# An attention and gate kernel: the projection's copies issued ahead of the scaling of o, head 0's copies of q and k made by engines instead of DMA, TensorE run on dummy matmuls during the first loads

## The chip, the cores and the metric

The kernel runs on one core of a Trainium2 chip. The metric is the time of one execution on the device, in microseconds (us). The core has five engines that run their own instruction queues in order: TensorE (PE; its weight loads are shown as PEld), VectorE (DVE), ScalarE (ACT), GpSimd (POOL) and SyncE (SP). Queues wait for one another by semaphores.

## The reference

`xn = layernorm(x)` with x of 2048 x 640. Attention over 32 heads of width 192 with cached k and v of 2048 rows, then a product with a gate that comes from a SwiGLU block on the same xn:

```python
def _A_ref(x, k_cache, v_cache, wq, wo):
    q = (x @ wq).reshape(B, Sq, 32, 192).transpose(0, 2, 1, 3)
    scores = einsum("bhqd,bhkd->bhqk", q, k_cache) * 192 ** -0.5
    o = einsum("bhqk,bhkd->bhqd", softmax(scores), v_cache)
    return o.transpose(0, 2, 1, 3).reshape(B, Sq, 32 * 192) @ wo
...
xn = _layernorm(A_x)
s = _A_ref(xn, k_cache, v_cache, wq, wo)
g = silu((silu(xn @ w1) * (xn @ w3)) @ w2)
return A_x + s * g
```

## The kernel before

Instructions stand on each engine in the order in which the program issues them. The work is a stream of (head h, block qb of 512 queries, pair p of key tiles): 32 x 4 x 8 steps. A step issues the scores two steps ahead and the values of its own pair. At the end of a block the kernel projects q of the next head for the same queries. Head 0 has no head in front of it, so its q is normalized and projected inside its own blocks.

```python
def project(h, qb, half):          # half 1 first, then half 0
    ...
    ps = ps_st.tile([P, 1024], F32, tag="st2", name="ps")     # one of TWO slots, shared with the scores
    for c in range(DC):
        nc.tensor.matmul(ps[:, 0:512], lhsT=w, rhs=xnT[:, c, qs], ...)
    if half:
        nc.scalar.copy(out=qAB[:, 1, qs], in_=ps[:, 0:512])
    else:
        nc.vector.tensor_copy(out=qAB[:, 0, qs], in_=ps[:, 0:512])
    nc.gpsimd.dma_start(out=qC[0:64, half, qs], in_=qAB[64:P, half, qs])
    if half == 0:
        nc.gpsimd.dma_start(out=qC[64:P, 0, qs], in_=qAB[0:64, 0, qs])

def values(n):
    ...                            # 16 matmuls into obank; behind the last pair of a block:
    nc.scalar.copy(out=osum[:], in_=ov[:, 0, :, 0:DH + 1])
    nc.vector.tensor_tensor(out=osum[:], in0=ov[:, 1, :, 0:DH + 1], in1=osum[:], op=ALU.add)
    nc.vector.reciprocal(out=rl, in_=osum[:, :, DH])
    nc.vector.tensor_tensor(out=ostage[...], in0=osum[:, :, 0:DH], in1=rl..., op=ALU.mult)

for n, (h, qb, p) in enumerate(stream):
    scores(n + 2)
    values(n)
    if h == 0 and qb + 1 < NQB:
        if p == 0 and qb > 0:
            ln_stats(qb + 1)       # VectorE: mean and variance of four tiles of x
        if p == NPAIR // 2 - 1:
            ln_norm(qb + 1)        # VectorE xn, TensorE transposes into a score slot, ScalarE copies to xnT
        if p == NPAIR - 3:
            project(0, qb + 1, 1)
            project(0, qb + 1, 0)
    if h + 1 < H:
        ...
        if p == NPAIR - 1:
            project(h + 1, qb, 1)
            project(h + 1, qb, 0)
    ...
```

The scores use the 192 rows of q and k as three rounds of 64 rows on both halves of the array. So some halves of q and k are needed on the other 64 partitions as well: these copies are qC and KC, and they are made by DMA. The other names in the views: `xn` is the normalized x and `pst` and `xnT` its transposes, `ps` a projection and `st` the scores (both in PSUM, the memory that TensorE writes to), `obank` the sums of the values, `osum` the addition of their two halves at the end of a block, `ostage` the scaled result.

## Time and profile before

| | before |
|---|---|
| time, median of 3 runs | 2080.41 us |
| span of the profiled run | 2077.2 us |
| TensorE busy | 1980.5 us (95%) |
| step of a steady block (osum addition to osum addition) | 13.38 us |
| first values matmul | 32.76 us |
| head 0's first three blocks | 20.6, 23.7, 23.8 us |

The first is the page of the profile: the line of the span, TensorE's line in the table of busy time (us, share, instructions), and the chain of work that ended last, by engine.

```profile
span 2077.2 us, 56883 instructions
...
PE 1980.5 (95%) x25838; PEld 1350.0 (65%) x25969; DVE 520.1 (25%) x850; ACT 1279.7 (62%) x1401; POOL 336.7 (16%) x575
...
PE 69%; DVE 16%; ACT 7%; issue 6%; DMA 1%; ACTq 0%; DVEq 0%; POOL 0%
```

VectorE is busy for a quarter of the span only, yet a sixth of the chain runs through it. Such a pair of numbers says: look for a short piece of VectorE work that TensorE waits for, over and over. It is found in the timeline at the end of a block (start us, duration us, engine, line, operation, output<-inputs, and in brackets the idle time of that engine just before and what ended it):

```profile
703.02 1.24 PE L293 MATMUL ps<-xnT,wq 128*128 128x512 bf16 x5
703.17 0.96 DVE L373 TENSOR_TENSOR osum<-obank,osum 128x772 f32<-128x772 f32 x1 [9.89 <-ACT osum L372]
...
704.17 0.18 DVE L375 RECIPROCAL rl_all<-osum 128x4 f32<-128x4 f32 x1
...
704.38 0.96 DVE L376 TENSOR_TENSOR ostage<-osum,rl_all 128x768 bf16<-128x768 f32 x1
...
704.85 0.83 PE L361 MATMUL obank<-vt_112,pT_11373 64*128 64x193 bf16 x16
...
705.26 0.68 DVE L297 CAST qAB<-ps 128x512 bf16<-128x512 f32 x1
...
705.99 0.37 PE L332 MATMUL st_11474<-qAB,KA 64*128 64x512 bf16 x1 [0.32 <-DVE qAB L297]
...
706.64 0.85 PE L361 MATMUL obank<-vt_112,pT_11398 64*128 64x193 bf16 x16
```

The projection is done near 704.2, but VectorE takes the reciprocal and scales o first, and casts qAB from 705.26 to 705.94. The next scores need the slot that the cast empties; they start at 705.99. The two lines of values are 1.79 us apart, where pairs in the middle of a block are 1.315 us apart. So 0.47 us are lost, once a block.

Head 0, next. The waits of TensorE from the start to the end of the first block, and in the second and third (who waited for whom, total us, times, longest us):

```profile
PE pst L276 <- DVE xn L273: 10.4, 2, 10.1
PE st_232 L332 <- DMA qC<-qAB: 6.2, 1, 6.2
PE st_232 L332 <- DMA KC<-KB: 4.0, 1, 4.0
PE st_460 L332 <- DMA qC<-qAB: 1.9, 1, 1.9
...
```

```profile
PE pst L276 <- DVE xn L273: 3.1, 4, 1.3
PE st_1062 L332 <- DMA qC<-qAB: 1.8, 1, 1.8
PE st_764 L332 <- DMA qC<-qAB: 1.8, 1, 1.8
PE st_764 L332 <- DVE qAB L297: 0.8, 1, 0.8
PE st_1062 L332 <- DVE qAB L297: 0.8, 1, 0.8
...
```

And head 0's first four blocks by windows of time: window, its length, busy us (and instructions) of PE, PEld, DVE, ACT and POOL, then the clock granted to TensorE as a share of full speed, DMA share, GB/s.

```profile
32.80:53.40 20.60, 17.35 (x206) 11.55 (x205) 1.54 (x4) 11.73 (x12) 2.66 (x5) 0.89 0.42 71
53.40:77.10 23.70, 18.95 (x215) 11.98 (x216) 9.71 (x25) 12.84 (x14) 4.68 (x8) 0.93 0.07 17
77.10:100.90 23.80, 19.02 (x215) 11.93 (x216) 9.73 (x24) 12.84 (x14) 4.68 (x8) 0.93 0.08 18
100.90:114.30 13.40, 13.03 (x187) 8.88 (x186) 3.31 (x6) 10.00 (x11) 4.19 (x6) 1.00 0.49 94
```

The clock is below 1.00 in the first three. After the wait for qC the score matmuls last about 0.6 us each instead of 0.38: TensorE has fallen back to half speed for a while (the granted clock is 0.50 from 47.64 to 51.06 us).

### The profile page before, as it was taken

Reading aid. Unit: us, or ns where it says so; the run is one execution under the profiler, and the core shown is the slowest. Engines: PE = TensorE matmul, PEld = TensorE weight load, DVE = VectorE, ACT = ScalarE, POOL = GpSimd, SP = SyncE. Lnnn points to the kernel's source line nnn. Section 1 sums busy time; section 2 is a strip of 40 time slices with the busy share of each in tenths; the row PEclk is TensorE's granted clock in tenths of the full one; section 3 lists DMA queues with packets and bytes.
Section 4 is the critical chain, followed back from the end, with each engine's and each line's share of the span. In section 5 each row is a group of like instructions: output and inputs, shape, how many; then the busy total and the mean of one; then the engine's idle time right before and its main releaser. Section 6 shows DMA issues by size and latency. Waiting matters only on the chain.

```text
span 2077.2 us, 56883 instructions
## 1 busy us (share of the span) xinstructions
PE 1980.5 (95%) x25838; PEld 1350.0 (65%) x25969; DVE 520.1 (25%) x850; ACT 1279.7 (62%) x1401; POOL 336.7 (16%) x575
## 2 busy tenths in 40 slices
PE   5899999999999999999999999999999999999998
PEld 2466666666666666666666666666666666567776
DVE  2422222222222222222222222222222222521111
ACT  3577777777777777777777777777777777220000
POOL 2111111111111111111111111111111110000000
PEclk8999999999999999999999999999999999999999
DMA  8033333433233323353433233232323230827772
GB/s 155 18 64 96 65 96 66 95 65 93 64 96 65 95 65 95 66 133 88 95 65 95 66 74 84 59 86 62 82 65 88 65 88 6 236 45 143 147 148 56
DMA packets 361848, 178.48 MB, mean 86 GB/s; under 512 B 307584, under 2 KB 348288, under 8 KB 361600
## 3 DMA queue, kind: packets, MB, share of 16 engines
q1 hardware_dynamic: 335984, 114.96, 25.6%
q0 software_dynamic: 23312, 57.18, 11.3%
q8 instruction: 205, 3.36, 0.7%
q10 hardware_dynamic: 2304, 2.62, 0.5%
q14 instruction: 43, 0.35, 0.1%
HBM read 54.66 MB, written 27.79 MB: 40 GB/s over the span
## 4 chain that ended last, share of the span: by engine, by line
PE 69%; DVE 16%; ACT 7%; issue 6%; DMA 1%; ACTq 0%; DVEq 0%; POOL 0%
PE obank L361 25%; PE ps_s L102 10%; DVE osum L373 6%; ACT osum L372 5%; DVE ostage L376 4%; DVE qAB L297 4%; PE ps_f L499 3%; DVE rl_all L375 1%; PE ps_gu L470 1%; PE ps_gu L473 1%; PE ps L293 1%; DVE stats L258 0%; DMA KC<-KB 0%; DMA qC<-qAB 0%; ACT xnT L278 0%
## 5 line engine op out<-in xcount | busy, mean ns | idle before, releaser
L373 DVE TENSOR_TENSOR osum<-obank,osum 128x772 f32<-128x772 f32 x128 | 123.1, 962 | 1264.4 <-ACT osum L372 1264.4
L298 POOL DMA_DIRECT2D qC<-qAB x256 | 136.4, 533 | 1372.9 <-ACT qAB L295 1170.5
L102 PE MATMUL ps_s<-wo_sb,oT 128*128 128x256 bf16 (+1 forms) x1536 | 210.5, 301 | 2.2 <-issue 2.2
L102 PEld LDWEIGHTS <-oT 128*128 128x128 bf16 x1536 | 150.7, 98 | 61.7 <-issue 3.9
L332 PEld LDWEIGHTS <-KC 64*128 64x128 bf16 x1024 | 96.3, 94 | 111.4 <-DMA KC<-KB 4.5
L293 PE MATMUL ps<-xnT,wqB 128*128 128x512 bf16 x513 | 154.8, 384 | 8.0 <-ACT xnT L278 1.3
L293 PE MATMUL ps<-xnT,wq 128*128 128x512 bf16 x640 | 159.4, 380 | 0.0
L333 PEld LDWEIGHTS <-KA 64*128 64x128 bf16 x1024 | 96.1, 94 | 59.7 <-issue 59.7
L332 PEld LDWEIGHTS <-KA 64*128 64x128 bf16 x1024 | 96.3, 94 | 58.3 <-issue 54.2
L376 DVE TENSOR_TENSOR ostage<-osum,rl_all 128x768 bf16<-128x768 f32 x128 | 122.6, 958 | 4.4
L293 PEld LDWEIGHTS <-wq 128*128 128x128 bf16 x640 | 62.8, 98 | 76.1 <-issue 1.1
L333 PEld LDWEIGHTS <-KB 64*128 64x128 bf16 x1024 | 96.9, 95 | 12.7 <-issue 12.7
L372 ACT COPY osum<-obank 128x772 f32<-128x772 f32 x128 | 101.9, 796 | 0.9 <-PE obank L361 0.9
L332 PEld LDWEIGHTS <-KB 64*128 64x128 bf16 x1024 | 96.5, 94 | 0.3 <-issue 0.3
L333 PEld LDWEIGHTS <-KC 64*128 64x128 bf16 x1024 | 96.6, 94 | 0.0
L293 PEld LDWEIGHTS <-wqB 128*128 128x128 bf16 x640 | 52.4, 98 | 67.6 <-issue 22.0
L297 DVE CAST qAB<-ps 128x512 bf16<-128x512 f32 x128 | 87.5, 683 | 23.5 <-PE ps L293 23.5
L295 ACT CAST qAB<-ps 128x512 bf16<-128x512 f32 x128 | 75.1, 586 | 13.8 <-PE ps L293 4.7
L300 POOL DMA_DIRECT2D qC<-qAB x128 | 67.1, 524 | 0.2 <-issue 0.2
L107 DVE SCALAR_TENSOR_TENSOR tmp<-ps_s,hT 128x384 f32<-128x384 f32 (+1 forms) x32 | 15.6, 487 | 181.3 <-PE ps_s L102 181.3
L499 PE MATMUL ps_f<-w_all,hT 128*128 128x384 bf16 (+1 forms) x384 | 52.3, 299 | 0.0
L98 POOL DMA_DIRECT2D xt<-in_A_x_dram x16 | 8.6, 540 | 257.6 <-DVE res L110 257.6
(9264 smaller groups left out, 5479.7 us busy)
## 6 DMA issues: line engine op xcount, KB each, us to landing
qC<-qAB POOLq DMA_DIRECT2D x384, 64.0 KB, 1.9
o_scr<-ostage SPq DMA_DIRECT2D x16, 1536.0 KB, 9.6
vt_112<-in_A_v_cache_dram SPq DMA_DIRECT2D x16, 768.0 KB, 6.5
vt_113<-in_A_v_cache_dram SPq DMA_DIRECT2D x16, 768.0 KB, 6.0
wq<-in_A_wq_dram POOLq DMA_DIRECT2D x32, 240.0 KB, 3.6
wo_sb<-in_A_wo_dram POOLq DMA_DIRECT2D x1, 7680.0 KB, 37.2
KC<-KA POOLq DMA_DIRECT2D x32, 128.0 KB, 5.8
KC<-KB POOLq DMA_DIRECT2D x32, 128.0 KB, 5.7
```

The lines of the kernel that those rows point to most:

```text
L102: nc.tensor.matmul(ps[:, b * 512:b * 512 + c1 - c0], lhsT=oT[:, k, :], rhs=wo_sb[:, k, c0:c1], start=(k == 0), stop=(k == OC - 1))
L293: nc.tensor.matmul(ps[:, 0:512], lhsT=w, rhs=xnT[:, c, qs], start=(c == 0), stop=(c == DC - 1))
L295: nc.scalar.copy(out=qAB[:, 1, qs], in_=ps[:, 0:512])
L297: nc.vector.tensor_copy(out=qAB[:, 0, qs], in_=ps[:, 0:512])
L298: nc.gpsimd.dma_start(out=qC[0:64, half, qs], in_=qAB[64:P, half, qs])
L332: nc.tensor.matmul(st2[:, 0:512], lhsT=k0, rhs=q0, start=r == 0, stop=r == 2)
L333: nc.tensor.matmul(st2[:, 512:1024], lhsT=k1, rhs=q1, start=r == 0, stop=r == 2)
L361: nc.tensor.matmul(obank[:, o0:o0 + DH + 1], lhsT=pT2[r * 64:(r + 1) * 64, t * 512 + j * P:t * 512 + (j + 1) * P], rhs=vt[r * 64:(r + 1) * ...
L372: nc.scalar.copy(out=osum[:], in_=ov[:, 0, :, 0:DH + 1])
L373: nc.vector.tensor_tensor(out=osum[:], in0=ov[:, 1, :, 0:DH + 1], in1=osum[:], op=ALU.add)
L376: nc.vector.tensor_tensor(out=ostage[:, qb * 4:qb * 4 + 4, hg * DH:(hg + 1) * DH], in0=osum[:, :, 0:DH], in1=rl.unsqueeze(2).to_broadcast( ...
L499: nc.tensor.matmul(ps[:, b * 512:b * 512 + c1 - c0], lhsT=hT[:, fc, i * P:(i + 1) * P], rhs=w2_sb[:, fc, c0:c1], start=(fc == 0), stop=(fc ...
```

## The change

Its intent: the cast that frees a score slot goes first; head 0 makes its partition-shifted copies by ScalarE and VectorE, straight out of PSUM for q, because a DMA is slow to land; head 0's projection comes one pair earlier; TensorE is kept busy from the start so that its clock is up when work arrives. The core of the diff:

```diff
 def copy_k(h):
-        nc.gpsimd.dma_start(out=KC[64:P, :], in_=KA[0:64, HK:SK])
-        nc.gpsimd.dma_start(out=KC[0:64, :], in_=KB[64:P, 0:HK])
+        if h == 0:
+            nc.scalar.copy(out=KC[64:P, :], in_=KA[0:64, HK:SK])
+            nc.scalar.copy(out=KC[0:64, :], in_=KB[64:P, 0:HK])
+        else:                                            # by DMA, as before
...
 def ln_norm(g):                                          # now ln_norm(g, i2): one half a call
-            nc.scalar.copy(out=xnT[...], in_=pst[:])
+        copy = nc.scalar.copy if i2 == 0 else nc.vector.tensor_copy
+        copy(out=xnT[...], in_=pst[:])
...
 def project(h, qb, half):
+        if h == 0 and half:
+            nc.vector.tensor_copy(out=qC[0:64, 1, qs], in_=ps[64:P, 0:512])
+        elif h == 0:
+            nc.scalar.copy(out=qC[0:64, 0, qs], in_=ps[64:P, 0:512])
+            nc.vector.tensor_copy(out=qC[64:P, 0, qs], in_=ps[0:64, 0:512])
+        else:                                            # by DMA, as before
...
-        nc.vector.reciprocal(...)                        # out of values(n)
-        nc.vector.tensor_tensor(out=ostage[...], ...)
+    def finish_values(h, qb):                            # the same two, called later
...
+    warm = ps_st.tile([P, 1024], F32, tag="st2", name="warm")
+    for i in range(56):
+        nc.tensor.matmul(warm[:, 0:P], lhsT=ident_bf[:], rhs=ident_bf[:], start=True, stop=True)
     load_x(0) ... load_k(0)
     ln_stats(0)
-    load_x(1)
     load_v(0)
-    for g in range(2, NQB):
+    for g in range(1, NQB):
...
-            if p == NPAIR // 2 - 1:                      # pair 3
-                ln_norm(qb + 1)
-            if p == NPAIR - 3:                           # pair 5
+            if p == NPAIR - 6:                           # pair 2
+                ln_norm(qb + 1, 0)
+            if p == NPAIR - 5:                           # pair 3
+                ln_norm(qb + 1, 1)
+            if p == NPAIR - 4:                           # pair 4
                 project(0, qb + 1, 1)
                 project(0, qb + 1, 0)
...
             project(h + 1, qb, 1)
             project(h + 1, qb, 0)
+        finish_values(h, qb)
```

More of the change, by code (lines that the diff above doesn't have):

```diff
@@ L228, in copy_k @@
         KC = kvp.tile([P, HK], BF16, tag="KC", name="KC")
-        nc.gpsimd.dma_start(out=KC[64:P, :], in_=KA[0:64, HK:SK])
-        nc.gpsimd.dma_start(out=KC[0:64, :], in_=KB[64:P, 0:HK])
+        if h == 0:
+            nc.scalar.copy(out=KC[64:P, :], in_=KA[0:64, HK:SK])
+            nc.scalar.copy(out=KC[0:64, :], in_=KB[64:P, 0:HK])
+        else:
+            nc.gpsimd.dma_start(out=KC[64:P, :], in_=KA[0:64, HK:SK])
+            nc.gpsimd.dma_start(out=KC[0:64, :], in_=KB[64:P, 0:HK])
         loads[h].update(KC=KC)
@@ L264, in ln_stats, with ln_norm @@
         lnorm[g] = (mv, rstd)
-    def ln_norm(g):
+    def ln_norm(g, i2):
         mv, rstd = lnorm[g]
-        for i2 in range(2):
-            pst = ps_st.tile([P, 2, DC, P], BF16, tag="st2", name="pst")
-            for k in range(2):
-                i = 2 * i2 + k
-                xn = lnp.tile([P, D], BF16, tag="xn", name="xn")
-                nc.vector.tensor_scalar(out=xn[:], in0=x_sb[:, 4 * g + i, :], scalar1=mv[:, i, 0:1], scalar2=rstd[:, i:i + 1],
-                                        op0=ALU.subtract, op1=ALU.mult)
-                for c in range(DC):
-                    nc.tensor.transpose(out=pst[:, k, c, :], in_=xn[:, c * P:(c + 1) * P], identity=ident_bf[:])
-            q0 = (4 * g + 2 * i2) * P
-            nc.scalar.copy(out=xnT[:, :, q0:q0 + 2 * P].rearrange("p c (k q) -> p k c q", k=2), in_=pst[:])
+        pst = ps_st.tile([P, 2, DC, P], BF16, tag="st2", name="pst")
+        for k in range(2):
+            i = 2 * i2 + k
+            xn = lnp.tile([P, D], BF16, tag="xn", name="xn")
+            nc.vector.tensor_scalar(out=xn[:], in0=x_sb[:, 4 * g + i, :], scalar1=mv[:, i, 0:1], scalar2=rstd[:, i:i + 1],
+                                    op0=ALU.subtract, op1=ALU.mult)
+            for c in range(DC):
+                nc.tensor.transpose(out=pst[:, k, c, :], in_=xn[:, c * P:(c + 1) * P], identity=ident_bf[:])
+        q0 = (4 * g + 2 * i2) * P
+        copy = nc.scalar.copy if i2 == 0 else nc.vector.tensor_copy
+        copy(out=xnT[:, :, q0:q0 + 2 * P].rearrange("p c (k q) -> p k c q", k=2), in_=pst[:])
     qtiles = {}
@@ L297, in project @@
             nc.vector.tensor_copy(out=qAB[:, 0, qs], in_=ps[:, 0:512])
-        nc.gpsimd.dma_start(out=qC[0:64, half, qs], in_=qAB[64:P, half, qs])
-        if half == 0:
-            nc.gpsimd.dma_start(out=qC[64:P, 0, qs], in_=qAB[0:64, 0, qs])
+        if h == 0 and half:
[4 more added lines that the diff above has]
+        else:
+            nc.gpsimd.dma_start(out=qC[0:64, half, qs], in_=qAB[64:P, half, qs])
+            if half == 0:
+                nc.gpsimd.dma_start(out=qC[64:P, 0, qs], in_=qAB[0:64, 0, qs])
     def swiglu(h, qb):
@@ L339, in _kernel_impl @@
     obanks = {}
+    osums = {}
     ostages = {}
@@ L365, in values @@
             return
-        hg = h % HG
-        if hg == 0 and qb == 0:
+        if h % HG == 0 and qb == 0:
             ostages[0] = stp.tile([P, NQT, HG * DH], BF16, tag="ostage", name="ostage")
-        ostage = ostages[0]
         ov = obank[:].rearrange("p (r j w) -> p r j w", r=2, j=4)
@@ L373, in values @@
         nc.vector.tensor_tensor(out=osum[:], in0=ov[:, 1, :, 0:DH + 1], in1=osum[:], op=ALU.add)
+        osums[0] = osum
+    def finish_values(h, qb):
+        osum, ostage, hg = osums[0], ostages[0], h % HG
         rl = rl_all[:, h * NQT + qb * 4:h * NQT + qb * 4 + 4]
@@ L408, in _kernel_impl @@
     ln_stats(0)
-    load_x(1)
     load_v(0)
-    for g in range(2, NQB):
+    for g in range(1, NQB):
         load_x(g)
-    ln_norm(0)
+    ln_norm(0, 0)
+    ln_norm(0, 1)
     project(0, 0, 1)
@@ L430, in _kernel_impl @@
                 ln_stats(qb + 1)
-            if p == NPAIR // 2 - 1:
-                ln_norm(qb + 1)
-            if p == NPAIR - 3:
+            if p == NPAIR - 6:
[3 more added lines that the diff above has]
+            if p == NPAIR - 4:
                 project(0, qb + 1, 1)
                 project(0, qb + 1, 0)
+        if p < NPAIR - 1:
+            continue
         if h + 1 < H:
-            if h == 0 and qb == 0 and p == NPAIR - 1:
+            if h == 0 and qb == 0:
                 copy_k(1)
-            if p == NPAIR - 1:
-                project(h + 1, qb, 1)
-                project(h + 1, qb, 0)
-        if p == NPAIR - 1:
-            if h < 2 * NPIG:
-                swiglu(h, qb)
-            loads_after(h, qb)
+            project(h + 1, qb, 1)
+            project(h + 1, qb, 0)
+        finish_values(h, qb)
+        if h < 2 * NPIG:
+            swiglu(h, qb)
+        loads_after(h, qb)
     att.close()
```

## The prediction

> **What bounds the kernel.** TensorE: 1980.5 of 2077.2 us busy in the page's table of engines. In steady heads the timeline shows the additions into osum on VectorE 13.38 us apart: one block of 512 queries each. A block is eight pairs, spaced 1.315 us, and ten projection matmuls; these need about 12.9 us. The rest is one stall. Timeline at 703 us: VectorE adds osum (703.17, 0.96 us), takes the reciprocal (0.18), scales o (704.38, 0.96), and only then casts qAB out of the second score slot (705.26 to 705.94), castable since about 704.3. TensorE finished the values of pair 0 at about 705.52 and started the next scores at 705.99, the wait being for qAB. Values of these two pairs start 1.79 us apart instead of 1.315: 0.47 us lost. The chain of waits agrees: it passes osum, reciprocal, ostage and the cast on VectorE (16% of the span).
>
> Head 0 is slower. Its first values start at 32.8 us; its first three blocks take 20.0, 23.7 and 23.8 us. The waits show why: scores wait 6.2 us for q's DMA copies (K's second load lands in that time too), then 4.0 for KC; each later projection of head 0 leaves TensorE waiting from 45.1 to 48.2 (cast, then qC by DMA), and the matmuls after it run at half speed for some 2.5 us. The Trainium skill (TensorE: Matmul & The Clock Gate, Part 1) has half rate after an idle window of about 3.4 us[...].
>
> **What the change does.**
> 1. The cast of qAB comes before reciprocal and scaling, in all 124 blocks with a projection. It can run at 704.3 to 705.0, before TensorE asks at 705.5, so all 0.47 us goes: 121 steady blocks, 57 us. Reciprocal and scaling come 0.7 us later; nothing soon waits for them. ScalarE's exp (1.02 us) still fits 1.315.
> 2. Start: copies of q and k by engines, an estimated 0.6 to 0.7 us each for q (from 586 and 683 ns for 128x512)[...], instead of 2 to 9 us by DMA. KC is ready near 20 us, bound by K's load; first values near 22.5 instead of 32.8: 10 us.
> 3. Head 0's blocks: no DMA wait, no slow clock, projection one pair earlier, half of the xnT copies on VectorE. But normalization comes one pair earlier, and its statistics on VectorE (4.5 us) end no sooner, so the wait for xn grows from 1.3 to about 2.3 us in two blocks. Net 5, 4.5 and 4.5: 14 us.
> 4. The 56 warm-up matmuls[...] end before xn is ready at 10 us: free, worth at most 2 us, inside item 2.
> 5. x's second block loads behind v: no cost, needed only near 26 us.
>
> The tail from 1768 us (309 us) and the last head, without projection, are unchanged.
>
> **Prediction.** 2080.4 - 57 - 10 - 14 = about 2000 us; range 1988 to 2024. Faster by over 2%: 0.94; within 2%: 0.05; slower: 0.01.
>
> **What would show it.** osum additions 12.9 us apart; no TensorE wait for qAB in steady blocks; first values at 21 to 24 us; no wait for qC or KC in head 0; its blocks near 15, 19 and 19 us at full clock; xn waits of about 2 us.
>
> **What would make it wrong.** A second limit just behind the stall: the cast not ready at 705.5 because projection or osum addition end later than read, or scores waiting for exp. In head 0: statistics holding TensorE over 3 us, so that the clock falls; ScalarE's queue held by KC's copy; x's second block late. None but the first exceeds 20 us.

## The result, and the profile after

| | before | after |
|---|---|---|
| time, median of 4 runs each | 2080.29 us | 2003.85 us (2002.45 to 2004.35) |
| ratio | | 0.9631 (95%: 0.9614 to 0.9648) |
| span of the profiled run | 2077.2 us | 2000.6 us |
| step of a steady block | 13.38 us | 12.88 us |
| first values matmul | 32.76 us | 23.15 us |
| head 0's first three blocks | 20.6, 23.7, 23.8 us | 17.9, 22.85, 22.85 us |

A ratio, here and below, is the mean time of one kernel's runs over the mean of the other's runs of the same rounds, so it is not quite the ratio of the medians quoted. The result is right on the reference's data, as are all the experiments.

The page after, the same lines:

```profile
span 2000.6 us, 57142 instructions
...
PE 1966.2 (98%) x26025; PEld 1306.8 (65%) x26025; DVE 529.0 (26%) x862; ACT 1280.0 (64%) x1403; POOL 329.5 (16%) x561
...
PE 97%; DVE 2%; ACT 1%; issue 0%; DMA 0%; POOL 0%; DVEq 0%; ACTq 0%
```

The chain is now TensorE almost from end to end. The end of a block in the timeline of the changed kernel:

```profile
627.70 1.24 PE L297 MATMUL ps<-xnT,wq 128*128 128x512 bf16 x5
627.86 0.96 DVE L383 TENSOR_TENSOR osum<-obank,osum 128x772 f32<-128x772 f32 x1 [9.28 <-ACT osum L382]
...
628.98 0.69 DVE L301 CAST qAB<-ps 128x512 bf16<-128x512 f32 x1 [0.15 <-PE ps L297]
...
629.53 0.83 PE L373 MATMUL obank<-vt_113,pT_10751 64*128 64x193 bf16 x16
629.59 0.17 DVE L389 RECIPROCAL rl_all<-osum 128x4 f32<-128x4 f32 x1
629.79 0.96 DVE L390 TENSOR_TENSOR ostage<-osum,rl_all 128x768 bf16<-128x768 f32 x1
...
630.20 0.38 PE L343 MATMUL st_10845<-qAB,KA 64*128 64x512 bf16 x1
...
630.85 0.83 PE L373 MATMUL obank<-vt_113,pT_10776 64*128 64x193 bf16 x16
```

The cast follows the osum addition, 0.15 us after it, when the projection is done. It ends at 629.67, and the scores at 630.20 wait for nothing. The values are 1.32 us apart.

Head 0's waits of TensorE after, from the start to the end of the first block, and then in the second and third:

```profile
PE pst L279 <- DVE xn L276: 3.0, 2, 2.7
PE warm L422 <- POOL ident_bf masks.py:199: 2.8, 1, 2.8
PE st_289 L343 <- ACT KC L231: 1.7, 1, 1.7
...
```

```profile
PE pst L279 <- DVE xn L276: 6.4, 2, 3.2
PE st_1119 L343 <- DVE qC L307: 0.6, 1, 0.6
PE st_821 L343 <- DVE qC L307: 0.6, 1, 0.6
...
```

No wait for a DMA is left. But where the second and third block waited 1.3 us for xn before, they wait 3.2 us now. The windows show that these two blocks gained only 0.9 us each, and that the clock is as low as it was:

```profile
23.20:41.00 17.80, 16.76 (x208) 11.10 (x205) 4.73 (x10) 11.18 (x12) 4.51 (x6) 0.92 0.62 130
41.00:63.90 22.90, 18.80 (x218) 11.38 (x216) 12.06 (x28) 12.49 (x14) 3.08 (x5) 0.93 0.04 10
63.90:86.70 22.80, 18.70 (x217) 11.51 (x216) 11.92 (x27) 12.29 (x14) 3.11 (x5) 0.93 0.05 10
86.70:99.60 12.90, 12.90 (x188) 8.54 (x186) 3.29 (x5) 10.00 (x11) 4.21 (x6) 1.00 0.49 104
```

Where the 76.6 us between the two spans lie, by marks read from both timelines:

| stretch | before | after | gain |
|---|---|---|---|
| start to first values | 32.76 | 23.15 | 9.6 |
| first values to first osum addition | 20.60 | 17.87 | 2.7 |
| second and third block | 47.54 | 45.70 | 1.8 |
| 122 further blocks, to 1733.50 and 1658.60 | 1632.60 | 1571.88 | 60.7 |
| last three blocks | 35.13 | 35.12 | 0.0 |
| output stage | 308.57 | 306.88 | 1.7 |

The last line is not of the change but chance. In the profile before, the granted clock is 0.50 for 3.4 us within the output stage (1860.1 to 1863.5 us); in the profile after it is not. The nine of all 13 profiles that have such a stretch there show an output stage of 307.7 to 309.0 us, the four without it 306.6 to 306.9, whatever the kernel.

### The profile page after: what moved, and what is told of

The parts are those of the page before. It is cut to its first block, busy times and chain, and to the rows that moved or that the text cites. A ratio compares the mean times of both kernels' runs of the same rounds, so it can differ in the third digit from the quotient of the medians.

```text
span 2000.6 us, 57142 instructions
## 1 busy us (share of the span) xinstructions
PE 1966.2 (98%) x26025; PEld 1306.8 (65%) x26025; DVE 529.0 (26%) x862; ACT 1280.0 (64%) x1403; POOL 329.5 (16%) x561
## 4 chain that ended last, share of the span: by engine, by line
PE 97%; DVE 2%; ACT 1%; issue 0%; DMA 0%; POOL 0%; DVEq 0%; ACTq 0%
PE obank L373 34%; PE ps L297 14%; PE ps_s L102 10%; PE ps_f L521 3%; PE ps_gu L492 1%; PE ps_gu L495 1%; DVE stats L262 0%; PE pst L279 0%; DMA x_all<-in_A_x_dram 0%; DVE qAB L301 0%; DVE osum L383 0%; ACT osum L382 0%; DVE mv L263 0%; ACT qC L306 0%; DVE qC L307 0%
## 5 line engine op out<-in xcount | busy, mean ns | idle before, releaser
L309 POOL DMA_DIRECT2D qC<-qAB x248 | 132.2, 533 | 1288.4 <-ACT qAB L299 1207.8
L297 PE MATMUL ps<-xnT,wqB 128*128 128x512 bf16 x640 | 161.4, 383 | 1.0 <-DVE xnT L282 1.0
L311 POOL DMA_DIRECT2D qC<-qAB x124 | 65.0, 524 | 0.3 <-issue 0.3
```

The lines of the kernel that those rows point to most:

```text
L297: nc.tensor.matmul(ps[:, 0:512], lhsT=w, rhs=xnT[:, c, qs], start=(c == 0), stop=(c == DC - 1))
```

## The experiments

Two theories had to be told apart. Theory A: the steady gain is the order of VectorE's queue alone, and head 0's blocks gained little because the statistics of x now hold TensorE for 3.2 us, after which it also runs at half speed. Rival B, in two parts: the steady gain needs the other parts, and head 0's blocks are held by the chain of copies out of the score slots. Eleven runs were made, of nine kernels. Three groups shared a chip and its runs of the kernel before: the order alone, all but the order, the copies by DMA, and the statistics earlier (before: median 2077.48 us); no warm-up, normalization later, the filled wait, and the changed kernel (2078.17); and the last three (2079.35).

### The order alone, and everything but the order

The first is the kernel before with only this:

```diff
         nc.vector.tensor_tensor(out=osum[:], in0=ov[:, 1, ...], in1=osum[:], op=ALU.add)
-        nc.vector.reciprocal(...)
-        nc.vector.tensor_tensor(out=ostage[...], ...)
...
         if p == NPAIR - 1:
+            finish_values(h, qb)      # the two, behind both projections
```

> The kernel before, with nothing changed but the place of the reciprocal and the scaling of o on VectorE: behind the cast of qAB. Theory A (the steady stall is the cast's late place in VectorE's queue, and nearly all of the gain comes from it): steady osum additions 12.88 to 12.90 us apart, 124 x 0.49 = 61 us less, time near 2019.5 (2017 to 2022); head 0's first values still at 32.8 us. Rival B (the gain needs the head-0 parts or the higher clock from warm-up, and the order alone moves the wait elsewhere): steps stay above 13.1 us, time above 2045.

Measured: 2019.59 us, ratio 0.9717 (0.9699 to 0.9736). The steps are 12.884 us on average, the same as in the changed kernel. First values came at 29.8 us, not at 32.8 as expected: the DMA copy of q held TensorE for 5.8 us here and KC for only 0.4 more, so the start by DMA varies by some us between runs. The time is within the expected range.

The second is the changed kernel with the two instructions put back:

```diff
+        finish_values(h, qb)
         if h + 1 < H:
             project(h + 1, qb, 1)
             project(h + 1, qb, 0)
-        finish_values(h, qb)
```

> The changed kernel, with the reciprocal and the scaling put back ahead of the projection's cast; all head-0 parts stay. Theory A: the steps go back to 13.38 us, 61 us lost, time near 2064 (2061 to 2068); first values still near 23.2 us. Rival B: steps below 13.2 us, time below 2045. With the first run this says whether the two parts add up: (before - first) + (before - this) should be 76.4 us to within 3.

Measured: 2060.45 us, ratio 0.9916 (0.9896 to 0.9937). The steps are 13.377 us again. First values came at 24.1 us, 0.9 later than expected. The time is 0.6 us under the expected range, probably for a reason that helps below: head 0's second and third block took 21.4 us instead of 22.85, at full clock.

```profile
40.60:62.00 21.40, 17.34 (x215) 10.85 (x216) 11.95 (x28) 12.40 (x14) 3.08 (x5) 1.00 0.05 11
62.00:83.40 21.40, 17.34 (x215) 10.86 (x216) 11.96 (x28) 12.29 (x14) 3.11 (x5) 1.00 0.05 11
```

TensorE gets to the transposes later there, by the stall, and waits 2.60 us for xn instead of 3.22. Together: the order alone gives 2077.48 - 2019.59 = 57.9 us, everything else 2077.48 - 2060.45 = 17.0; the sum, 74.9, is the change's 76.4 to within 1.5 us. The first part of B falls.

### The copies of head 0

The changed kernel with head 0's copies of q and k by DMA again:

```diff
-        if h == 0:                    # KC by ScalarE
+        if False:
...
-        if h == 0 and half:           # qC by VectorE
+        if False:
-        elif h == 0:                  # qC by ScalarE and VectorE
+        elif False:
```

> The changed kernel, with head 0's copies of q and k by DMA again, all else kept. Theory A (the copies by engine gain at the start; in the blocks the wait for statistics decides): first values 7 to 10 us later than 23.2; blocks of head 0 from osum to osum change by under 1.5 us from 22.85, because the projection stands one pair earlier and the wait for xn is still there; time near 2012 (2010 to 2015). Rival B (the copies are what saves head 0's blocks too): each of the first three blocks gets 2.5 us longer or more, with waits of TensorE for qC by DMA of 1.5 us or more, time 2017 or more.

Measured: 2015.76 us, ratio 0.9693 (0.9674 to 0.9712); this is 0.8 us above the expected range. The changed kernel was not run in this group; its first runs gave 2003.85, and a later group on the same chip 2004.35. First values at 34.8 us, 11.6 us later than by engine in the profile after, more than the 7 to 10 expected: TensorE waited 11.1 us for qC. The copies stand on another queue than the loads of k, v and x, but on the same 16 DMA engines, which moved 207 GB/s from 17 to 30 us; they took 11.3 us to land, against a median of 1.9 us over the whole run before. That the traffic is the cause is argued, not shown. The blocks came to 18.35, 23.67 and 23.39 us: 0.5 to 0.8 us longer. Waits for qC came back (3.3 us over the second and third block), and the wait for xn was 3.2 us as in the changed kernel. So the copies by engine are worth what they give at the start, and little in the blocks. The second part of B is weakened, not yet refuted.

### The warm-up

```diff
-    for i in range(56):
+    for i in range(1):
         nc.tensor.matmul(warm[:, 0:P], ...)
```

> The changed kernel with one warm-up matmul in place of 56. Theory A (they are off the chain that bounds the start, which is the load of K, the copies of q and KC): first values at 23 to 24.5 us, time within 2 us of the changed kernel run beside it. Rival (warm-up is worth its own share): first values later by 2 us or more.

Measured: 2003.68 us; the changed kernel beside it 2004.35. First values at 24.5 us, and at 24.4 in the changed kernel's profile beside it. The 56 matmuls gain nothing. In the profile after they run from 2.77 to 7.3 us, and they do bring the clock up: they start 0.107 us apart until 5.5 us and 0.056 from there. TensorE then idles 2.75 us until xn, the granted clock is 0.50 again from 12.30 to 15.72 us, and the first projection runs at half speed all the same (its first five matmuls of 512 columns start 0.42 us apart, against 0.22 in a steady block).

### The statistics earlier

The changed kernel, with the statistics of the next but one block's first two tiles behind head 0's projection, where VectorE has some 4 us free, and only the other two where all four stood:

```diff
             if p == 0 and qb > 0:
-                ln_stats(qb + 1)
+                ln_stats(qb + 1, (2, 3))
...
                 project(0, qb + 1, 0)
+                if qb + 2 < NQB:
+                    ln_stats(qb + 2, (0, 1))
```

> The changed kernel, with the statistics of x's blocks 2 and 3 split: two of four tiles at the end of the previous block, where VectorE has some 4 us free before the osum addition, the other two where all four stood. Theory A (head 0's blocks gained only 0.9 us each because TensorE waits 3.2 us for xn behind the statistics and then runs at half speed for about 4 us): the wait falls to about 1 us, granted clock in these blocks goes to 1.00, blocks go from 22.85 to about 19 (18.3 to 19.7), time near 1996 (1994.5 to 1998). Rival B (the blocks are held by the chain of copies out of the score slot by ScalarE and VectorE): blocks stay above 21.5 us, time above 2001.

Measured: 1996.04 us, ratio 0.9601 (0.9583 to 0.9619). The wait for xn is 0.99 us a block, the clock 1.00, the blocks 19.30 us each:

```profile
PE pst L288 <- DVE xn L285: 2.0, 2, 1.0
...
41.50:60.80 19.30, 17.16 (x215) 10.75 (x216) 12.06 (x28) 12.39 (x14) 3.32 (x6) 1.00 0.12 25
```

All as theory A has it; the copies out of the score slots were not touched, so they did not hold these blocks at 22.85.

### Normalization one pair later

```diff
-            if p == NPAIR - 6:        # pair 2
+            if p == NPAIR - 5:        # pair 3
                 ln_norm(qb + 1, 0)
```

> The changed kernel with the first half of the normalization back at pair 3, where the kernel before had it; the projection stays at pair 4. Theory A (bringing normalization one pair forward made TensorE wait 3.2 us for xn, long enough to lose the full clock): the wait falls by one pair to 1.9 us, the clock stays full, the second and third block go from 22.85 to 20 to 21 us, time 4 to 6 us below the changed kernel beside it. Rival B (the copies out of the score slots hold these blocks): blocks above 22 us, time within 1.5 us of it.

Measured: 2000.39 us, 4.0 below the changed kernel beside it. The wait is 1.91 us in both blocks. One block behaved as expected, the other did not:

```profile
41.00:63.20 22.20, 18.73 (x216) 11.56 (x216) 11.99 (x28) 12.49 (x15) 3.08 (x5) 0.92 0.05 10
63.20:83.80 20.60, 17.19 (x215) 10.80 (x216) 11.95 (x28) 12.38 (x15) 3.11 (x5) 1.00 0.05 12
```

With the same wait, the clock fell in one and stayed full in the other. That pair is a clean price of the slow clock: 22.14 against 20.60 us by the osum additions, 1.5 us. It also says that the length of the wait alone does not decide it.

### Filling the wait

Same wait, but TensorE busy in it:

```diff
         pst = ps_st.tile([P, 2, DC, P], BF16, tag="st2", name="pst")
+        if g > 1 and i2 == 0:
+            for f in range(44):
+                nc.tensor.transpose(out=pst[:, 0, 0, :], in_=ident_bf[:], identity=ident_bf[:])
```

> The changed kernel with 44 transposes of the identity, whose result is overwritten, in front of the first transposes of x in blocks 2 and 3, so that TensorE works through most of the wait for xn. xn is not ready any sooner. Theory A' (half of what is lost there is the slow clock after the wait, and it goes if TensorE is kept busy): the granted clock in these blocks stays near 1.00, blocks go from 22.85 to 21.0 to 21.6 us, time 2.5 to 3.7 us below the changed kernel beside it. Rival (only the wait costs, the clock does not): blocks stay at 22.6 us or more.

Measured: 2001.56 us, 2.8 below the changed kernel beside it. xn is ready no sooner (the transposes of x start at 49.38 us, as against 49.37 after), and the blocks take 21.5 us at full clock:

```profile
41.00:62.60 21.60, 19.80 (x260) 13.21 (x260) 12.00 (x28) 12.40 (x15) 3.08 (x5) 1.00 0.05 11
62.60:84.10 21.50, 19.68 (x259) 13.21 (x260) 11.93 (x28) 12.27 (x14) 3.11 (x5) 1.00 0.05 11
```

So of the 22.85 us, 1.3 are the slow clock. The rest adds up: 21.52 less the 2.23 us by which the earlier statistics shortened the wait is 19.29, and it measured 19.30.

### The changed kernel beside these

> The changed kernel itself once more, to stand beside the other three on the same chip: ratio to the kernel before 0.963 (0.9614 to 0.9648 in its first runs), first values near 23.2 us, blocks 22.85 us.

Measured: 2004.35 us, ratio 0.9641 (0.9623 to 0.9659). First values at 24.4 us, later than expected by 1.2, and blocks of 24.0 us instead of 22.85, at a granted clock of 0.86 in these windows instead of 0.93, with the same wait of 3.22 us. How long the clock stays low varies from run to run: here 6.8 us in the second block (48.7 to 55.5 us), in the first profile 3.4 us (49.9 to 53.3).

### Three tiles early, and both beside the changed kernel once more

The last step takes three of the four tiles early, 3.3 us of work into the 4 us that are free:

```diff
-                ln_stats(qb + 1, (2, 3))
+                ln_stats(qb + 1, (3,))
...
-                    ln_stats(qb + 2, (0, 1))
+                    ln_stats(qb + 2, (0, 1, 2))
```

> As the run with two of four tiles' statistics early, but three of four: 3.3 us of work into VectorE's 4 us free before the osum addition. Theory A (each us of statistics taken from in front of xn is a us off TensorE's wait, until the wait is gone): the remaining wait for xn of 0.99 us falls to 0 to 0.2 us, blocks 2 and 3 go from 19.30 to 18.3 to 18.6 us, time about 2 us below that run beside it. If the early statistics delay the osum addition or the cast behind it, the gain is eaten there: blocks at 19.3 or more, and a TensorE wait for qAB or osum appears.

> The run with two of four tiles early once more, beside the others: about 8 us below the changed kernel beside it (7 to 9), blocks of 19.3 us.

> The changed kernel once more, beside the other two: 2003 to 2005 us; blocks 2 and 3 at 22.8 to 24.0 us, depending on how long the clock stays low.

Measured, five runs each on one chip: three early 1993.06 us (1992.66 to 1994.62), ratio 0.9588 (0.9572 to 0.9604); two early 1995.35; changed 2002.03 (2001.74 to 2003.41), ratio 0.9630. With three tiles early no wait for xn is left, no new wait for osum or qAB appears, and the blocks are 18.30 us: 0.99 less than with two early, which is the whole wait that was left.

```profile
41.00:59.30 18.30, 17.25 (x217) 10.75 (x216) 12.08 (x28) 12.40 (x14) 3.31 (x6) 1.00 0.12 27
59.30:77.60 18.30, 17.26 (x217) 10.74 (x216) 8.87 (x18) 12.29 (x14) 2.42 (x4) 1.00 0.05 13
```

This version beats both kernels: it is 9.0 us below the changed one beside it. Two early is 6.7 below instead of the 7 to 9 expected, and the changed kernel at 2002.03 came 1 us under its range. In its profiled run (2003.41 us, the slowest of the five) it kept its clock in one of the two blocks; whether the other four did so too is not on record:

```profile
42.00:64.90 22.90, 18.80 (x218) 11.39 (x216) 11.99 (x28) 12.48 (x14) 3.08 (x5) 0.93 0.04 10
64.90:86.40 21.50, 17.25 (x217) 10.75 (x216) 11.93 (x28) 12.29 (x14) 3.12 (x5) 1.00 0.05 11
```

The second line has a wait of 3.21 us, no filler, and the 21.5 us of the filled kernel: what the slow clock costs is 1.3 us there, whichever way it is avoided.

## Why the prediction was right, and where it was wrong

1. **What bounds the kernel, and the steady blocks: right.** Predicted 12.9 us a step and 57 us in all; measured 12.88 us and 60.7 us. The stall was named, its size read from two lines of values (0.47 us), and the measured saving is 13.38 - 12.88 = 0.50 us; 122 steps from the third block on, not 121, make the rest. The kernel with this alone gives 57.9 us, the change without it 17.0.
2. **The start: right in size.** Predicted 10 us and first values near 22.5; measured 9.6 us and 23.15 (24.4 and 24.0 in the repeats). With the copies by DMA again, first values came at 34.8 us. But the start of the kernel before varies too (32.8 us, and 29.8 with the order alone), so a single pair of profiles gives the gain to some us only. KC was ready near 20.1 us, as predicted, but not for the reason given, "bound by K's load": that was luck. The two loads of K landed near 11.8 and 13.1 us; ScalarE's copies of KC (1.04 us each) began at 18.00, as soon as ScalarE had cast qC (17.39 to 17.97). The chain of the start in the profile runs from the load of x's first block through its statistics and the first projection to these copies.
3. **Head 0's blocks: wrong in size.** This is the step that failed: "Net 5, 4.5 and 4.5: 14 us." The profile shows 2.7 for the first block and 1.8 for the other two, together 4.5 us. Two terms in it were off in the second and third block. The prediction put the wait for xn at "about 2.3 us"; it is 3.2. Its own numbers gave this: the statistics end no sooner, TensorE comes to the transposes one pair (1.315 us) and one stall (0.47 us) earlier, so 1.3 + 1.3 + 0.5 = 3.1 us. And it put these blocks at full clock ("no slow clock"); the granted clock is 0.93, as before. What it listed as a danger, "statistics holding TensorE over 3 us, so that the clock falls", is what happened. The fall of the clock moved from behind the wait for qC to behind the wait for xn. The filled kernel prices the clock at 1.3 us a block, and the early statistics price the wait at 1 us a us. So the two terms make 1.3 + 0.9 = 2.2 of the 3.6 us by which each of these blocks fell short; the prediction does not itemize its 4.5, and the other 1.4 us stay open. The first block took 17.87 us against "near 15" (and 20.6 before, where the prediction read 20.0): it began at half clock, until 25.96 us, and took 16.49 in the two runs whose clock was full from its start (everything but the order, and no warm-up); the rest there stays open too.
4. **The warm-up: right that it is free; its worth is nothing.** Allowed "at most 2 us"; measured 2003.68 without against 2004.35 with.
5. **The load order of x and v, the last head, the tail: right.** The statistics of x's second block asked for their load at 18.7 us, not near 26, and waited 0.31 us, in the shadow of the start. The last three blocks took 35.13 and 35.12 us.

The total, 2000 predicted and 2003.85 measured, is good partly because errors of opposite sign met: 4 us too little on the steady blocks, 9.5 us too much on head 0's. That is luck, as are the 1.7 us of the output stage.

What decides whether the clock falls is not the length of the wait alone. Directly behind a wait of 3.2 us it fell in nine of the ten second and third blocks seen (with both sets of copies), after 2.6 us in none of two, after 1.9 us in one of four, after 1.3 us or less in none of eight. No experiment was made for the clock's rule, but the 13 traces show most of it. Over short stretches the granted clock is either 1.00 or 0.50, and within each trace it changes only at points that lie whole multiples of 3.413 us apart. In the profile after:

```profile
46.44:49.85 3.41, 0.48 (x8) 0.41 (x8) 3.09 (x11) 0.17 (x1) 1.50 (x2) 1.00 0.00 0
49.85:53.26 3.41, 3.41 (x30) 2.00 (x29) 0.89 (x2) 2.25 (x2) 0.02 (x1) 0.50 0.00 0
```

Cut every trace at these points, from the first one on, and take the share of each stretch in which TensorE was busy, transposes included (rough, since the ends of matmuls are modelled). At full clock, all 35 stretches that were busy for 42% or less were followed by half clock, none of the 7472 that were busy for 50% and more, and 14 of the 27 between. At half clock, none of the 22 stretches that were busy for up to 78% was followed by full clock, and all 46 that were busy for 80% and more were. So a wait costs the clock when it leaves one such stretch empty enough, and where the points lie differs from run to run. In the changed kernel's repeat, the stretch from 48.69 to 52.11 us, at half clock, was busy for 2.66 us, 78%, and a second at half clock followed; the block took 24.0 us. In the filled kernel, the stretch from 45.08 to 48.50 us was busy throughout, but only 1.1 us of it were matmuls; without the transposes it would be among those after which the clock fell. The two blocks with normalization later lie between the limits (1.62 us busy, and the clock fell; 1.51 us, and it did not), and what decides there stays open.

## What to carry to other kernels

When an engine that is a quarter busy shows up in the chain of waits, look at the order of its queue at that point: an instruction that frees a buffer belongs ahead of work that nobody waits for yet, and here that order alone gave 58 of 76 us. When a change brings a consumer forward, add up how much earlier it arrives at each producer that does not move; the wait that disappears at one place is otherwise found again at the next. Take a gap on TensorE at more than its length, because the clock may be low behind it (here 1.3 us behind a wait of 3.2); a cheap test is to fill the gap with matmuls that do nothing.

## What the Trainium skill lacked or had wrong

- "TensorE: Matmul & The Clock Gate", Part 1, has the clock fall after at least one idle window of about 3.4 us, and says that the window runs freely. The runs agree with the window: all changes of the clock within a trace lie on one grid of 3.413 us, which sits differently in each run. But the stretch before a fall need not be idle: in the kernel before, TensorE was busy for 1.35 of the 3.41 us from 44.23 to 47.64, and the clock was 0.50 after it; it fell after all 35 stretches that were busy for 42% or less.
- The same page, Part 4, says that transposes do not count as busy in the same way for the clock. Here they seem to count: with 44 of them in the wait of 3.2 us, the clock stayed at 1.00 in both blocks, where it fell in nine of ten without. And with the copies by DMA, the stretch from 61.15 to 64.56 us, at half clock, was busy for 3.09 us, only 1.9 of them matmuls, and full clock followed, as it did after no stretch at half clock that was busy for 2.66 us or less in all.
- The same page, Part 1, counts the warm-up as time of sustained work. It lacks that the clock so gained can be lost to a gap under one window with short transposes behind it: after 4.5 us of matmuls came a gap of 2.75 us, the stretch from 8.89 to 12.30 us was busy for 1.62 us with transposes, and the first projection ran at half speed (0.42 us between matmuls of 512 columns).
- "DMA: Bandwidth & Descriptors", Anatomy of one DMA, gives a fixed cost of about 2 us for a copy issued by GpSimd. The median of the 64 KB copies of q agrees (1.9 us), but beside the loads of k, v and x the same copies took 6.4 us (before) and 11.3 us (with the changed order of loads). That section does not give the time of such copies in the traffic of bulk loads.
